# Where weights are asked for, and how side work is slotted, in the backward pass of a gated attention and MLP block

## The chip, the cores and the metric

The kernel runs on one core of one Trainium2 chip. The core has a matrix engine (PE, with weight loads PEld beside it), a vector engine (DVE), a scalar engine (ACT), GpSimd (POOL) and SyncE (SP), which here only issues transfers. Transfers run on 16 DMA engines; SP's transfers show as queue q1, POOL's as q0, ACT's as q10. The metric is the device time of one execution in microseconds, the median of several runs.

## The reference

The forward pass mixes an attention block and an MLP with a scalar gate, for one token of width D = 640:

```python
x = A_x
g = _sigmoid((x * gate_w).sum(-1, keepdims=True))
a = _A_ref(x, A_k_cache, A_v_cache, A_wq, A_wo)
b = _B_ref(x, B_w1, B_b1, B_w2)
return g * a + (1 - g) * b
```

`_A_ref` is attention of one query per head over a cache: 32 heads, 4096 keys, head width 128, bf16. `_B_ref` is `x @ w1 + b1`, then `h * tanh(softplus(h))`, then `@ w2`, with a hidden width of 1728. The kernel must return the output and, for an incoming gradient `grad_out`, the gradients of x, the K cache, the V cache, wq, wo, w1, b1, w2 and gate_w. The K and V caches are 32 MB each and are read once; their gradients are as large and are written once. The gradient of K is an outer product per head (a column ds over the keys, times q), that of V likewise (the column p, times the gradient of the head's output).

## The kernel before

Heads are taken two at a time: a pair n is one tile `Kn` and one tile `Vn` of 128 partitions by 64 by 128, 2 MB each. There are 16 pairs, and the main loop runs `period(n, mid)` for each. Four heads form a group g (two pairs), which has its rows of wo (`wo_g`, 640 KB); eight heads share a slice of wq (`wq_g`, 1280 KB).

A period does this for its pair. PE transposes V in eight chunks (`V(c)`: `transposes`, L606, evicted by ACT to `tT`, L608) and multiplies each with the head's output gradient (`dP(c)`, L615). In the meantime DVE takes the maximum of the scores (L695, the first DVE instruction of a period), ACT makes the exponentials, PE sums them (L710), and PE forms the output O (L732). DVE then makes `part`, `dd` and `dm` (L741, L750, L752), and ACT spreads dm to `ds` (L761). PE multiplies K with dm (L768). The K of the next pair is transposed (`K(c)`) and its scores are formed (`SC(c)`) in the second half of the period. The large DVE work is `outer` (L638): the gradient of V is written over the tile Vn in four quarters (`dv_part`), that of K over Kn in the next period (`dk_part`). After the last quarter POOL issues the store, and SP the load that takes the freed buffer: `load_k(n + 4)` (four buffers) and `load_v(n + 3)` (three buffers). So on SP each K or V load waits until the store of the pair that had the buffer has landed, and what is behind it on SP waits too. Pairs 3 and 9 store V in six pieces (`spread`).

All other work is in a list of named steps with dependencies (`add(name, kind, fn, deps, head)`): kind P for PE, D for DVE, T for anything that is not counted. `slot(h, p, d)` stands at six places of a period, and takes from the list, in its order, up to p steps of kind P and d of kind D whose dependencies were done in an earlier slot; the default is two and one. Step groups:

- `prep_steps(g)` (added by `mid(n)` of the period before the group's first): DVE's products of wo_g with the output gradient (`do_part`, L290), PE's q from wq_g (`qbc`, L301), and the small steps that make the group's vectors.
- `finish_steps(g)` after a group's second pair: the output's product with wo_g (L377), the gradient of wo written over wo_g (`dwo`, L385) and stored by POOL (L386), the query gradient's part of dx from wq_g (`dx`, L396).
- `mlp_steps()`: h and its activation; then, in pieces `CH` of w2's row blocks, the forward product (`b_part`, L496), `dh_part` (L507), the gradient of w2 written over the piece (`dw2_part`, L516, L519); then `dh_cast` and `dh_bc_part` (L540, an ACT copy of dh's rows to all partitions), `dx_part` (L550) and `dw1_part` (L557).

Weights: SP asks for the first two wq_g, the first three wo_g, w1 and the first two pieces of w2 in the beginning. The later two wq_g and five wo_g are asked for on ACT: wq_g by a step after the last `dx` that reads the old one, wo_g by `mid(n)` of odd periods. A wo_g load waits until the store of the gradient that was in its buffer has landed (three buffers). The rows `dh_bc` share their tag, and so their two buffers, with the pieces of w2.

An instruction that waits holds up all that is behind it on its engine, and the order on each engine is that of the program text, slots included.

Of the kernel before, what the change touches and what calls it, by code (L numbers as in the profile page):

```python
# [11 lines left out]
BF16 = mybir.dt.bfloat16  # L12
# [4 lines left out]
def kernel(  # L17
# [39 lines left out]
    FB = FM * P  # L57
    FR = F - FB
    FCN = FM + 1
    CH = [(0, 4), (4, 7), (7, 10), (10, FCN)]  # L60
    NCH = len(CH)
    NT = J // 8
    scale = float(Dh) ** -0.5
# [62 lines left out]
            vts[n] = kv_in.tile([P, J, Dh], BF16, name="Vn", tag="Vn", bufs=VB)  # L126
            nc.sync.dma_start(vts[n][:], Vv[n])

    def load_wq(w, q=nc.sync):
        if w < H // WG:  # L130
            wqs[w] = wts.tile([P, RC, WG * Dh], BF16, name="wq_g", tag="wq_g")
            q.dma_start(wqs[w][:], wq_v[:, :, w * WG * Dh:(w + 1) * WG * Dh])

    def load_wo(g, q=nc.sync):
        if g < NG:
            wos[g] = wts.tile([P, G, D], BF16, name="wo_g", tag="wo_g", bufs=3)
            q.dma_start(wos[g][:], wo_v[g])

    w2cs = {}

    def load_w2(c):
        a, b = CH[c][0], min(CH[c][1], FM)
        w2cs[c] = mlp.tile([P, 4, D], BF16, name="w2c", tag="w2c", bufs=2)
        nc.sync.dma_start(w2cs[c][:, 0:b - a, :], w2_v[:, a:b, :])

    load_wq(0)
# [114 lines left out]
    def add(name, kind, fn, deps=(), head=0):  # L261
        steps.append((name, kind, fn, tuple(deps), head))
# [89 lines left out]
    def finish_steps(g):  # L352
        fs = {}

        def om():
            fs["om"] = small.tile([P, G, G], BF16, name="om", tag="om")
            nc.vector.tensor_tensor(fs["om"][:], o_all[:, g * G:(g + 1) * G].unsqueeze(2).to_broadcast([P, G, G]),
                                    mask4[:].to_broadcast([P, G, G]), ALU.mult)

        def o4():  # L360
            fs["ps"] = gr_ps.tile([P, G], F32, name="o4_ps", tag="gr")
            R = P // G
            for hh in range(G):
                nc.tensor.matmul(fs["ps"][hh * R:(hh + 1) * R, :], lhsT=red4[:], rhs=fs["om"][:, hh, :],
                                 start=True, stop=True)

        def o4c():
            fs["o4"] = small.tile([P, G], F32, name="o4", tag="o4")
            nc.vector.tensor_copy(fs["o4"][:], fs["ps"][:])
            fs["o4b"] = small.tile([P, G], BF16, name="o4b", tag="o4b")  # L370
            nc.vector.tensor_copy(fs["o4b"][:], fs["o4"][:])

        def amm():
            fs["ap"] = gr_ps.tile([P, RC], F32, name="ap_ps", tag="gr")
            for c in range(RC):
                for i in range(G):
                    nc.tensor.matmul(fs["ap"][:, c:c + 1], lhsT=wos[g][:, i, c * P:(c + 1) * P],  # L377
                                     rhs=fs["o4b"][:, i:i + 1], start=(i == 0), stop=(i == G - 1))

        def aadd():  # L380
            nc.vector.tensor_tensor(a_acc[:], a_acc[:], fs["ap"][:], ALU.add)

        def dwo():
            for i in range(G):
                nc.vector.tensor_scalar(wos[g][:, i, :], da_bc[:], fs["o4"][:, i:i + 1], None, ALU.mult)  # L385
            (nc.sync if g == NG - 1 else nc.gpsimd).dma_start(dwo_v[g], wos[g][:])  # L386

        def dqb():
            b_ps = gr_ps.tile([P, G, P], BF16, name="b_ps", tag="gr")
            bcast_rows(b_ps, dq_all[:, g * G:(g + 1) * G], G)  # L390
            nc.scalar.copy(f32v(dq_bc[:, g * GD:(g + 1) * GD]), f32v(b_ps[:].rearrange("p a b -> p (a b)")))

        def dx(rc, c0, c1, slot_i):
            def f():
                w = g // 2
                nc.vector.scalar_tensor_tensor(junk[:, c0:c1], in0=wqs[w][:, rc, c0:c1], scalar=1.0,  # L396
                                               in1=dq_bc[:, w * WG * Dh + c0:w * WG * Dh + c1],
                                               op0=ALU.mult, op1=ALU.mult, accum_out=dxp[:, rc, slot_i:slot_i + 1])
            return f

        n = lambda x: f"{x}{g}"
        add(n("om"), "T", om)
        add(n("dqb"), "P", dqb)
        add(n("o4"), "P", o4, (n("om"),))
        add(n("o4c"), "T", o4c, (n("o4"),))
        add(n("amm"), "P", amm, (n("o4c"),))
        add(n("aadd"), "T", aadd, (n("amm"),))
        add(n("dwo"), "D", dwo, (n("aadd"),))
        for rc in range(RC):
            if g >= NG - 2:  # L410
                add(n(f"dx{rc}_"), "D", dx(rc, (g % 2) * GD, (g % 2 + 1) * GD, g - NG + 2 + NW - 1), (n("dqb"),))
            elif g % 2 == 1:
                add(n(f"dx{rc}_"), "D", dx(rc, 0, WG * Dh, g // 2), (n("dqb"),))
        if g % 2 == 1 and g < NG - 2:
            add(n("wql"), "T", lambda: load_wq(g // 2 + 2, nc.scalar), (n(f"dx{RC - 1}_"),))


    def mlp_steps():
# [107 lines left out]
        def dh_cast():  # L526
            m["dh_bf"] = T("dh_bf", BF16)
            nc.vector.tensor_copy(m["dh_bf"][:], m["dh"][:])
            m["dh_bc"] = mlp.tile([P, F], BF16, name="dh_bc", tag="w2c", bufs=2)

        def dh_bc_part(k):
            def f():
# [33 lines left out]
        for c in range(NCH):  # L566
            add(f"b{c}", "P", b_part(c), ("act2", f"w2_{c}") + ((f"badd{c - 1}",) if c else ()), H0)
            add(f"badd{c}", "T", b_add, (f"b{c}",), H0)
            a, b = CH[c]
            for fc in range(a, b):  # L570
                add(f"dh_{fc}", "D", dh_part(fc), ("act2", f"w2_{c}"), H0)
            add(f"dw2a_{c}", "D", dw2_part(c, a, a + 2), (f"badd{c}",) + tuple(f"dh_{fc}" for fc in range(a, b)), H0)
            add(f"dw2_{c}", "D", dw2_part(c, a + 2, b), (f"dw2a_{c}",), H0)
            if c < 2:
                done[f"w2_{c}"] = -1
            else:
                for k in range(4):
                    add(f"w2w{k}_{c}", "T", lambda: None, (f"w2w{k - 1}_{c}" if k else f"dw2_{c - 2}",), H0)
                add(f"w2l_{c}", "T", lambda c=c: load_w2(c), (f"w2w3_{c}",), H0)
                for k in range(8):  # L580
                    last = k == 7
                    add(f"w2_{c}" if last else f"w2x{k}_{c}", "T", lambda: None,
                        (f"w2x{k - 1}_{c}" if k else f"w2l_{c}",), H0)
        add("dhc", "T", dh_cast, (f"dh_{FCN - 1}", f"dw2_{NCH - 2}"), H0)
        add("dhb0", "P", dh_bc_part(0), ("dhc",), H0)
        add("dhb1", "P", dh_bc_part(1), ("dhc",), H0)
        for rc in range(RC):
# [89 lines left out]
    def period(n, mid):  # L677
# [29 lines left out]
            nc.scalar.activation(pairs(e[hp, :, k]), own(S, k, hp), ACT.Exp, bias=negM[hp], scale=1.0)  # L707
        V(3)
        dP(1)
        nc.tensor.matmul(Z, lhsT=ones_bf[:], rhs=e[:].rearrange("p j k -> p (j k)"), start=True, stop=True)  # L710
        zs = small.tile([P, 2], F32, name="zs", tag="zs")
        nc.vector.reduce_sum(zs[:], Z.rearrange("p (j k) -> p k j", k=2), axis=AX.X)
        rz = st["rz"] = small.tile([P, 2], F32, name="rz", tag="rz")
        nc.vector.reciprocal(rz[:], zs[:])
        dk_part(n - 1, 2)
        V(4)
        dP(2)
        slot(2 * n)
        p_bf = st["p"] = small.tile([P, J, 2], BF16, name="p_bf", tag="p_bf", bufs=2)
        for k, hp in HS:  # L720
            nc.scalar.activation(p_bf[hp], e[hp, :, k].unsqueeze(2).to_broadcast([HP, J, 2]), ACT.Copy,
# [3 lines left out]
        dk_part(n - 1, 3)  # L725
        V(6)
        dP(4)
        slot(2 * n)
        V(7)
        dP(5)  # L730
        for j in range(J):
# [2 lines left out]
            if j == J // 2 - 1:  # L734
                dP(6)
        dP(7)
        slot(2 * n, 2, 2)
        part = small.tile([P, 1], F32, name="part", tag="part")
        pj = f32v(junk[:])[:, 0:J]
        for k, hp in HS:  # L740
# [10 lines left out]
        for k, hp in HS:  # L751
            nc.vector.scalar_tensor_tensor(pairs(dm[hp, :, k]), in0=own(DP, k, hp), scalar=dd[hp],  # L752
                                           in1=pairs(p_bf[hp, :, 0]), op0=ALU.subtract, op1=ALU.mult)
        dv_part(n, 1)
        mid(n)
        nc.vector.tensor_tensor(o_all[:, 2 * n:2 * n + 2], O[:, 0:2], rz[:], ALU.mult)
        ds = st["ds"] = small.tile([P, J, 2], BF16, name="ds_bf", tag="ds_bf", bufs=2)
        SC(0)
        K(2)
        for k, hp in HS:  # L760
            nc.scalar.copy(ds[hp], dm[hp, :, k].unsqueeze(2).to_broadcast([HP, J, 2]))  # L761
        dv_part(n, 2)
        slot(2 * n + 1)
        SC(1)
        K(3)
        dv_part(n, 3)
        for j in range(J):
            nc.tensor.matmul(DQ, lhsT=kts[n][:, j, :], rhs=dm[:, j, :].unsqueeze(1).to_broadcast([P, W // 2, 2]),  # L768
                             start=(j == 0), stop=(j == J - 1))
            if j == J // 2 - 1:  # L770
                SC(2)
                K(4)
                slot(2 * n + 1)
                SC(3)
                K(5)
        SC(4)
# [34 lines left out]
    def mid(n):  # L811
        g = n // 2
        if n % 2 == 0 and g + 1 < NG:
# [1 line left out]
            steps.clear()  # L815
            prep_steps(g + 1, 2 * n + 1)
            steps.extend(rest)
        if n % 2 == 1:
            assert g == 0 or f"dwo{g - 1}" in done
            if g:  # L820
                load_wo(g + 2, nc.scalar)
        if n == NP - 2:
            for rc in range(RC):
                add(f"dwq{rc}", "D", dwq_make(rc), (f"dqb{NG - 2}",), 2 * n + 1 + (rc + 1) // 2)
                add(f"dwqs{rc}", "T", lambda rc=rc: dwq_store(rc), (f"dwq{rc}",), 2 * n + 1)

    for n in range(NP):
        period(n, mid)
        if n % 2 == 1:
            mlp_left = steps[:]  # L830
            steps.clear()
            finish_steps(n // 2)
            steps.extend(mlp_left)
# [78 lines left out]
```

## Time and profile before

| | us |
|---|---|
| median of 8 runs | 416.01 (414.9 to 417.65) |
| the profiled execution | 415.71 |
| its span, first to last instruction | 413.9 |

| engine | busy us (share of the span) |
|---|---|
| PE | 295.0 (71%) |
| PEld | 262.8 (63%) |
| DVE | 309.3 (75%) |
| ACT | 201.4 (49%) |
| POOL | 32.6 (8%) |

The granted clock of the matrix engine was 0.895 in the mean. The transfers by queue, with packets, bytes and the time of their packets as a share of 16 engines' span:

```profile
q1 hardware_dynamic: 10208, 87.51, 52.0%
q0 software_dynamic: 7040, 70.64, 41.5%
q10 hardware_dynamic: 2092, 5.91, 4.0%
```

The costliest groups of DVE, which carries the outer products and most of the side work (line, engine, operation, written tile from read tiles with their shapes, count, then busy us and mean ns of one, then the idle time just before them and what ended most of it):

```profile
L638 DVE TENSOR_TENSOR Vn<-p_bf,qd 128x2048 bf16<-128x2048 bf16 x64 | 78.0, 1220 | 1.0
L638 DVE TENSOR_TENSOR Kn<-ds_bf,qd 128x2048 bf16<-128x2048 bf16 x64 | 77.5, 1218 | 0.9
L290 DVE SCALAR_TENSOR_TENSOR junk<-wo_g,da_bc 128x640 bf16<-128x640 bf16 x32 | 26.3, 821 | 15.5 <-DMA wo_g<-in_A_wo_dram 13.8
```

In the page's slice rows one digit or number stands for a fortieth of the span (10.3 us). In the list of waits a line says which instruction waited for what, then the us in total, the number of times, and the longest.

### The profile page before, as it was taken

The page shows a single profiled execution, that of the slowest core. Times are in us where ns is not written, and L with a number is a line of the kernel's source. Part 1 is how long each engine was busy: PE and PEld are TensorE (multiplying, and loading weights), DVE is VectorE, ACT ScalarE, POOL GpSimd, SP SyncE. Part 2 cuts the span into 40 slices and gives each one's busy share as a digit, 9 for nine tenths or more (in the row PEclk, how much of TensorE's full clock was granted, in tenths as well). Part 3 has the DMA queues.
Part 4 walks back from the last instruction along what each step waited for, and adds up shares of the span by engine and source line. Part 5 has one row for each costly group of instructions (what it writes and reads, how often), then busy time and mean ns, then how long its engine had stood idle before and what let it go on. Part 6 is the DMA issues. An engine that isn't in the chain of part 4 may idle for free.

```text
span 413.9 us, 13164 instructions
## 1 busy us (share of the span) xinstructions
PE 295.0 (71%) x5665; PEld 262.8 (63%) x5672; DVE 309.3 (75%) x736; ACT 201.4 (49%) x451; POOL 32.6 (8%) x72
## 2 busy tenths in 40 slices
PE   1799788686788868537977788836887778978410
PEld 0578788586676758427866677725776667868300
DVE  3318766885499995807769969992799999989983
ACT  1475646372464735404755365705747455737100
POOL 1000100011200000101000102211000010001000
PEclk9899999999698977858999889986999989999755
DMA  8999999999999999998999999999999999998997
GB/s 304 423 415 398 421 412 429 426 429 426 420 415 382 392 415 426 426 401 311 388 355 432 422 420 316 409 356 425 423 380 393 422 414 415 421 405 360 403 420 286
DMA packets 19398, 164.90 MB, mean 398 GB/s; under 512 B 2300, under 2 KB 3004, under 8 KB 11404
## 3 DMA queue, kind: packets, MB, share of 16 engines
q1 hardware_dynamic: 10208, 87.51, 52.0%
q0 software_dynamic: 7040, 70.64, 41.5%
q10 hardware_dynamic: 2092, 5.91, 4.0%
q8 instruction: 44, 0.72, 0.7%
q14 instruction: 14, 0.11, 0.1%
HBM read 82.03 MB, written 82.03 MB: 396 GB/s over the span
## 4 chain that ended last, share of the span: by engine, by line
issue 36%; DMA 25%; DVE 22%; PE 9%; ACT 3%; POOL 2%; SPq 1%; POOLq 0%; ACTq 0%; DVEq 0%
DMA Kn<-in_A_k_cache_dram 9%; DMA Vn<-in_A_v_cache_dram 7%; DVE Vn L638 5%; DVE Kn L638 5%; DMA out_dram<-w2c 5%; PE tr L606 3%; DMA out_dram<-Kn 3%; DVE junk L396 2%; ACT tT L608 2%; DVE junk L550 2%; DMA wq_g<-in_A_wq_dram 2%; PE sB L768 1%; PE sA L615 1%; DVE junk L290 1%; DVE dwq_t L793 1%
## 5 line engine op out<-in xcount | busy, mean ns | idle before, releaser
L608 ACT COPY tT<-tr 128x512 f32<-128x512 f32 x256 | 144.9, 588 | 121.3 <-PE tr L606 106.2
L615 PEld LDWEIGHTS <-tT 128*128 128x128 bf16 x2048 | 81.1, 99 | 40.9 <-ACT tT L608 34.2
L606 PE MATMUL tr<-ident_f,Kn 128*128 128x128 f32 x512 | 88.3, 300 | 3.8 <-DMA Kn<-in_A_k_cache_dram 1.9
L606 PE MATMUL tr<-ident_f,Vn 128*128 128x128 f32 x512 | 78.8, 284 | 0.0
L638 DVE TENSOR_TENSOR Vn<-p_bf,qd 128x2048 bf16<-128x2048 bf16 x64 | 78.0, 1220 | 1.0
L638 DVE TENSOR_TENSOR Kn<-ds_bf,qd 128x2048 bf16<-128x2048 bf16 x64 | 77.5, 1218 | 0.9
L615 PE MATMUL sA<-qd,tT 128*128 128x48 bf16 x1024 | 49.1, 188 | 23.7 <-ACT tT L608 22.7
L606 PEld LDWEIGHTS tr<-ident_f,Vn 128*128 128x128 f32 x512 | 57.0, 145 | 9.4 <-PE sB L615 7.9
L606 PEld LDWEIGHTS tr<-ident_f,Kn 128*128 128x128 f32 x512 | 60.1, 152 | 4.3 <-issue 2.2
L615 PE MATMUL sB<-qd,tT 128*128 128x48 bf16 x1024 | 47.0, 184 | 2.4 <-issue 1.1
L290 DVE SCALAR_TENSOR_TENSOR junk<-wo_g,da_bc 128x640 bf16<-128x640 bf16 x32 | 26.3, 821 | 15.5 <-DMA wo_g<-in_A_wo_dram 13.8
L768 PEld LDWEIGHTS <-Kn 128*128 128x128 bf16 x1024 | 33.4, 100 | 6.7 <-issue 6.1
L768 PE MATMUL sB<-dm,Kn 128*128 128x48 bf16 x1024 | 33.8, 189 | 4.9 <-DVE dm L752 3.1
L732 PE MATMUL sA<-em,Vn 128*128 128x48 bf16 x1024 | 30.9, 183 | 0.7 <-issue 0.7
L695 DVE TENSOR_REDUCE m<-sA 64x1 f32<-64x64 f32 x32 | 7.1, 221 | 30.1 <-PE sA L615 29.8
L732 PEld LDWEIGHTS <-Vn 128*128 128x128 bf16 x1024 | 28.0, 96 | 0.8 <-issue 0.8
L396 DVE SCALAR_TENSOR_TENSOR junk<-wq_g,dq_bc 128x1024 bf16<-128x1024 bf16 (+1 forms) x25 | 25.1, 1006 | 0.2
L301 PE MATMUL q_ps<-wq_g,cols_bf 128*128 128x512 bf16 x33 | 12.1, 489 | 11.5 <-DMA wq_g<-in_A_wq_dram 10.6
L662 POOL DMA_DIRECT2D out_dram<-Vn x13 | 7.1, 545 | 166.4 <-DVE Vn L638 87.1
L741 DVE SCALAR_TENSOR_TENSOR junk<-sB,em 64x64 f32<-64x64 f32 x32 | 7.1, 222 | 17.4 <-PE sB L615 8.4
L650 POOL DMA_DIRECT2D out_dram<-Kn x15 | 8.4, 560 | 134.9 <-DVE m L325 43.8
L745 PE MATMUL sB<-ident_f,part 128*128 128x128 f32 x16 | 5.0, 310 | 14.8 <-DVE junk L741 14.6
(150 smaller groups left out, 265.5 us busy)
## 6 DMA issues: line engine op xcount, KB each, us to landing
Kn<-in_A_k_cache_dram SPq DMA_DIRECT2D x16, 2048.0 KB, 13.7
Vn<-in_A_v_cache_dram SPq DMA_DIRECT2D x16, 2048.0 KB, 16.9
out_dram<-Kn POOLq DMA_DIRECT2D x15, 2048.0 KB, 15.5
out_dram<-Vn POOLq DMA_DIRECT2D x13, 2048.0 KB, 15.3
out_dram<-wo_g POOLq DMA_DIRECT2D x7, 640.0 KB, 15.3
out_dram<-dwq_t SPq DMA_DIRECT2D x4, 896.0 KB, 10.8
wo_g<-in_A_wo_dram ACTq DMA_DIRECT2D x5, 640.0 KB, 14.0
wq_g<-in_A_wq_dram SPq DMA_DIRECT2D x2, 1280.0 KB, 6.3
```

The costliest lines, as they stand in the source:

```text
L290: nc.vector.scalar_tensor_tensor(junk[:, 0:D], in0=wos[g][:, i, :], scalar=1.0, in1=da_bc[:], op0=ALU.mult, op1=ALU.mult, accum_out=gp["do ...
L301: nc.tensor.matmul(q_ps[:], lhsT=x_bf[:, rc:rc + 1].to_broadcast([P, P]), rhs=wq[:, rc, off:off + GD], start=(rc == 0), stop=(rc == RC - 1))
L396: nc.vector.scalar_tensor_tensor(junk[:, c0:c1], in0=wqs[w][:, rc, c0:c1], scalar=1.0, in1=dq_bc[:, w * WG * Dh + c0:w * WG * Dh + c1], op ...
L550: nc.vector.scalar_tensor_tensor(junk[:, 0:F // 2], in0=w1_sb[:, rc, a:b], scalar=1.0, in1=m["dh_bc"][:, a:b], op0=ALU.mult, op1=ALU.mult, ...
L606: nc.tensor.transpose(tp[:, t, :], flat[:, k * P:(k + 1) * P], ident_f[:])
L608: nc.scalar.copy(sb[:].rearrange("p a b -> p (a b)"), tp[:].rearrange("p a b -> p (a b)"))
L615: nc.tensor.matmul(out[:, 4 * k:4 * k + W], lhsT=tb[:, t, par, :], rhs=vec[:, par].rearrange("p k r -> p (k r)").unsqueeze(1).to_broadcast ...
L638: nc.vector.tensor_tensor(dst[:, a:b, :].rearrange("p j (a b) -> p j a b", b=2), col[:, a:b, :].unsqueeze(2).to_broadcast([P, n, Dh // 2, 2]),
L650: ring(n).dma_start(dKv[n], kts[n][:])
L662: ring(n).dma_start(dVv[n], vts[n][:])
L732: nc.tensor.matmul(O, lhsT=vts[n][:, j, :], rhs=e[:, j, :].unsqueeze(1).to_broadcast([P, W // 2, 2]), start=(j == 0), stop=(j == J - 1))
L768: nc.tensor.matmul(DQ, lhsT=kts[n][:, j, :], rhs=dm[:, j, :].unsqueeze(1).to_broadcast([P, W // 2, 2]), start=(j == 0), stop=(j == J - 1))
```

## The change

- The pieces of w2 are three row blocks each (five pieces) instead of four, three, three and four (four pieces), and their buffers are smaller.
- `load_wq` and `load_wo` always issue on SP. The wo_g load of an odd period stands ahead of the period, hence ahead of that period's K load on SP, instead of in `mid(n)`.
- `dh_bc` has a tag and a buffer of its own, and `dh_cast` depends only on the last dh, not on the gradient of the last but one piece of w2.
- Four slots take two steps of DVE instead of one, so that all six take two. The third slot of a period moves from ahead of `part` to behind `dm`, and `mid(n)` stands right behind it, ahead of the second quarter of dV.
- `V(4)` goes ahead of the sum of exponentials, and `K(2)` ahead of `SC(0)`.

```diff
-    CH = [(0, 4), (4, 7), (7, 10), (10, FCN)]
+    CH = [(0, 3), (3, 6), (6, 9), (9, 12), (12, FCN)]
...
-    def load_wq(w, q=nc.sync):
+    def load_wq(w):
...
-            q.dma_start(wqs[w][:], wq_v[:, :, w * WG * Dh:(w + 1) * WG * Dh])
+            nc.sync.dma_start(wqs[w][:], wq_v[:, :, w * WG * Dh:(w + 1) * WG * Dh])
-    def load_wo(g, q=nc.sync):
+    def load_wo(g):
...
-            q.dma_start(wos[g][:], wo_v[g])
+            nc.sync.dma_start(wos[g][:], wo_v[g])
...
-        w2cs[c] = mlp.tile([P, 4, D], BF16, name="w2c", tag="w2c", bufs=2)
+        w2cs[c] = mlp.tile([P, 3, D], BF16, name="w2c", tag="w2c", bufs=2)
...
-            add(n("wql"), "T", lambda: load_wq(g // 2 + 2, nc.scalar), (n(f"dx{RC - 1}_"),))
+            add(n("wql"), "T", lambda: load_wq(g // 2 + 2), (n(f"dx{RC - 1}_"),))
...
-            m["dh_bc"] = mlp.tile([P, F], BF16, name="dh_bc", tag="w2c", bufs=2)
+            m["dh_bc"] = mlp.tile([P, F], BF16, name="dh_bc", tag="dh_bc")
...
-            add(f"dw2a_{c}", "D", dw2_part(c, a, a + 2), (f"badd{c}",) + tuple(f"dh_{fc}" for fc in range(a, b)), H0)
-            add(f"dw2_{c}", "D", dw2_part(c, a + 2, b), (f"dw2a_{c}",), H0)
+            add(f"dw2a_{c}", "D", dw2_part(c, a, a + 1), (f"badd{c}",) + tuple(f"dh_{fc}" for fc in range(a, b)), H0)
+            add(f"dw2_{c}", "D", dw2_part(c, a + 1, b), (f"dw2a_{c}",), H0)
...
-        add("dhc", "T", dh_cast, (f"dh_{FCN - 1}", f"dw2_{NCH - 2}"), H0)
+        add("dhc", "T", dh_cast, (f"dh_{FCN - 1}",), H0)
...
         dP(1)
+        V(4)
         nc.tensor.matmul(Z, lhsT=ones_bf[:], rhs=e[:].rearrange("p j k -> p (j k)"), start=True, stop=True)
...
         dk_part(n - 1, 2)
-        V(4)
         dP(2)
-        slot(2 * n)
+        slot(2 * n, 2, 2)
...
         dP(4)
-        slot(2 * n)
+        slot(2 * n, 2, 2)
...
         dP(7)
-        slot(2 * n, 2, 2)
         part = small.tile([P, 1], F32, name="part", tag="part")
...
+        slot(2 * n, 2, 2)
+        mid(n)
         dv_part(n, 1)
-        mid(n)
...
+        K(2)
         SC(0)
-        K(2)
...
         dv_part(n, 2)
-        slot(2 * n + 1)
+        slot(2 * n + 1, 2, 2)
...
                 K(4)
-                slot(2 * n + 1)
+                slot(2 * n + 1, 2, 2)
...
-        if n % 2 == 1:
-            assert g == 0 or f"dwo{g - 1}" in done
-            if g:
-                load_wo(g + 2, nc.scalar)
...
     for n in range(NP):
+        g = n // 2
+        if n % 2 == 1:
+            assert g == 0 or f"dwo{g - 1}" in done
+            if g:
+                load_wo(g + 2)
         period(n, mid)
```

## The prediction

> **What bounds the kernel now.** I read the page first: busy shares, then the forty slices. No engine is full (DVE, the busiest, 75%), while the DMA row stands at 8 or 9 in every slice.
>
> ```profile
> DMA  8999999999999999998999999999999999998997
> GB/s 304 423 415 398 421 412 429 426 429 426 420 415 382 392 415 426 426 401 311 388 355 432 422 420 316 409 356 425 423 380 393 422 414 415 421 405 360 403 420 286
> DMA packets 19398, 164.90 MB, mean 398 GB/s; under 512 B 2300, under 2 KB 3004, under 8 KB 11404
> ```
>
> So the transfers bound it: 164.90 MB at the rate of a good slice would need 390 us (164.90 / 0.423), and the rest of the span is the start, the end and the slices that dip. Next I cut the span at the dips. Columns: stretch and length, busy us of PE, PEld, DVE, ACT, POOL, granted clock, DMA share, GB/s.
>
> ```profile
> 130.00:140.00 10.00, 9.04 (x197) 8.32 (x197) 9.79 (x25) 5.95 (x15) 1.09 (x2) 1.00 1.00 357
> 140.00:185.00 45.00, 28.88 (x513) 25.42 (x514) 29.73 (x69) 18.15 (x41) 2.67 (x5) 0.76 1.01 423
> 185.00:195.00 10.00, 7.92 (x151) 7.38 (x149) 5.92 (x16) 3.92 (x11) 0.53 (x1) 0.84 0.79 288
> ...
> 205.00:220.00 15.00, 11.91 (x238) 10.99 (x237) 10.67 (x22) 9.25 (x21) 0.53 (x1) 1.00 1.00 369
> ...
> 245.00:255.00 10.00, 7.70 (x167) 6.95 (x167) 9.40 (x24) 6.05 (x13) 0.53 (x1) 1.00 0.89 303
> ...
> 265.00:280.00 15.00, 7.25 (x159) 6.54 (x157) 13.35 (x34) 3.56 (x8) 1.66 (x3) 0.86 1.01 364
> ...
> 300.00:320.00 20.00, 15.78 (x322) 13.92 (x319) 19.40 (x41) 11.40 (x26) 1.06 (x2) 1.00 0.98 385
> ...
> 370.00:380.00 10.00, 7.29 (x135) 6.87 (x135) 9.45 (x20) 5.25 (x12) 1.95 (x3) 1.00 0.85 347
> ```
>
> Against 423 GB/s a stretch loses its length times (1 - rate/423): 1.6, 3.2, 1.9, 2.8, 2.1, 1.8 and 1.8 us in the order shown (the second row is the reference), and 0.4 more in 195 to 205 (405 GB/s). Together 15.6 us: all that a change of order can win, since it moves as many bytes. Why do they dip? I asked for the waits inside two windows (170 to 192, 268 to 290).
>
> ```profile
> DVE junk L290 <- DMA wo_g<-in_A_wo_dram: 13.8, 1, 13.8
> PE q_ps L301 <- DMA wq_g<-in_A_wq_dram: 10.6, 1, 10.6
> ```
>
> ```profile
> ACT dh_bc L540 <- DMA out_dram<-w2c: 11.9, 1, 11.9
> PEld L615 <- ACT tT L608: 11.2, 1, 11.2
> ```
>
> In both the computing engines stand still; no dK or dV store is asked for, hence no load into the buffer that it would free, and some us later the DMA runs dry. A third kind: ACT blocks on an issue of its own, and its copies behind it wait.
>
> ```profile
> 104.79 0.37 ACTq L137 DMA_DIRECT2D wo_g<-in_A_wo_dram  x1
> 105.25 0.58 ACT L608 COPY tT<-tr 128x512 f32<-128x512 f32 x1 [5.15 <-DMA out_dram<-wo_g]
> ```
>
> Why did the wq_g load, issued on ACT at 143.2, land only at 182? The DMA view of 144 to 182 says it (queue: packets, MB, share):
>
> ```profile
> q0 software_dynamic: 731, 7.73, 48.2%
> q1 hardware_dynamic: 453, 6.64, 41.0%
> q10 hardware_dynamic: 726, 1.66, 11.1%
> ```
>
> q10, ACT's queue, got as many packets as q0 and a fifth of the bytes. I lastly timed the periods by the reduce of L695: they start at 24.8, 42.9, 63.1, 87.1, 113.3, 137.0, 161.1, 194.8, 214.5, 242.0, 261.8, 293.1, 313.7, 337.0, 356.0 and 376.3. The long ones, period 6 (33.7 us) and 10 (31.3), hold the two stalls; an undisturbed one is 18 to 24 us.
>
> **What the Trainium skill says.** "DMA: Bandwidth & Descriptors", Queues, rings and completion order: each DMA engine goes round robin over the queues that have work, one packet each. The counts above agree (731 against 726). Same page, Anatomy of one DMA: DMA engines don't wait on semaphores, the wait sits on the issuing sequencer before dispatch. The 5.15 us above agree. Same page, Issuing engines are not separate DMA queues: a second issuer brings no bandwidth; the total here stays near 423 with three queues at work.
>
> **The change part by part.**
>
> Weights to SyncE. Two wq_g and five wo_g loads leave ACT for SP's queue q1. ACT's 9.9 us of blocking (three waits in the list of waits) go. On q1 a load follows the K and V loads in line. wq_g of groups 4 and 5 is asked for behind V of pair 7, at about 149 (V of pair 7 was issued at 149.2). It needs V's time to land (16.9 us, median) and some 3 us of its own (1.31 MB at 423), so about 168; the first use was tried at 171.6 and will come a few us sooner without ACT's stalls. I take the 10.6 and 13.8 us waits as gone but for a rest of 1 or 2 us; from the trace it could be 0 or the full 10. SP is in order, so each added issue can hold what is behind it. A wo_g load waits for the wo_g store two groups back (136.2 for the load in period 5); that store follows the dV store (133.1) on POOL's queue, whose end SP has already waited for with V. The K load behind waits for the dK store of 144.6, which is later. So nothing behind is held beyond 1 to 2 us; the issue itself takes 0.33 to 0.43. wq_g's own release, five DVE reads, is long past. The w2c loads wait for w2c stores one to two periods old: nothing.
>
> dh rows in their own buffer. The 11.9 us wait on the w2c store goes, and with it ACT's 11.2 us for PE. The rows also come out behind the ds copies on ACT. What is late next: DVE, which idles only 8.3 us there.
>
> DVE work two to a slot, and the third slot behind dm. By instruction count the total is the same to 3 rows; only the place changes. Prices from rows of the before, with the accumulator read: L396 1.30, L507 0.96, L290 0.90, L550 1.13, L385 and L516 0.38, L557 0.66. In the built order period 4 gets 2 L507, 1 L396 and 1 L516 more (3.6 us), period 8 1 L507, 1 L396 and 3 L516 (3.4), period 12 1 L396 and 1 L550 (2.4); periods 9 and 13 lose 6 to 7 us each, and fall under what PE and ACT need anyway (18 to 20 us, as periods 0, 7 and 13 show), so that isn't all given back. In period 4 some 3.5 us of it stand ahead of the dV store. Cover: period 4 was filled by DVE (23.0 of 23.7 us), so there is none on DVE; the cover is the queued transfers. I charge 0.4 us each, 1.2 in all; 0 if the queues stay full, 3.5 each if they are dry. The slot behind dm brings dm, ds and PE's dQ forward by two L396 at most; worth nothing where the DMA is the bound.
>
> V(4) ahead of the Z matmul: PE waits there 9.4 us in all for ACT's exp, 0.6 a period; hidden by the DMA as well. w2 by threes: one piece more, same bytes. On POOL's queue two w2c stores now stand ahead of a dK and a dV store, 0.49 MB each, 1.2 us later for those; inside the cover of the queued transfers, so nothing; without it 2.4.
>
> **Sum.** Of each dip I take what its cause carries. 185 to 205: 3.2 of 3.6 (the weights stall). 205 to 220: 1.6 of 1.9 (period 7's stores came late from it). 245 to 255: 1.2 of 2.8 (two stores lay far apart, 234.3 and 249.8, in a period of 27.4 us that period 8's added work doesn't shorten). 265 to 280: 1.0 of 2.1 (it begins ahead of the dh wait). 300 to 320: 1.4 of 1.8 (follows from that wait). 370 to 380: 0.6 of 1.8 (loads are over, period 13 is lighter). 130 to 140: nothing (period 4 grows). Sum 9.0, less 1.2, so 7.8. The profiled span 413.9 becomes 406.1; its execution took 415.71, 1.8 beyond the span, so 407.9; the median shown is 416.01, 0.3 more: 408. A measurement of this kernel tells about 0.3% (1.2 us) from no change.
>
> **Rivals.**
> Full recovery, chance 0.22. Without their stalls (5, 4, 13, 4 and 10 us in periods 3, 5, 6, 8 and 10) the periods add up to 336 of 372 us, well under what the DMA needs; then compute waits for loads and the queues never empty: 416.0 - 15.6 = 400.4. Against it: K loads let PE wait only 1.9 us so far, and bunched work dries queues locally.
> The gaps move, chance 0.10. Stores now come in bunches after periods 4, 8 and 12 and the DMA dries there instead: 9.0 won, three times 3 lost, 416.
> Slower, chance 0.18: wq_g is the head of q1 while POOL's stores fill q0. Its 2 KB packets, 40 on each engine, each let one q0 packet by. From the rows above a q10 packet took 0.09 us and a q0 packet 0.40 (share x 38 us x 16 / packets), so 40 pairs take 20 us, not 3, and K and V loads stand behind it for 17 us, twice. It also lands too late again, so of the gains only the dh parts (2.4) stay. If a quarter of 34 us reaches the end: 416.0 - 2.4 + 1.2 + 8.5 = 423. It decides once wq_g lands more than 22 us after its issue (149 to 171). For it: the 39 us on q10. Against it, the window 58 to 68, where wq_g ran on q1 beside stores:
>
> ```profile
> q1 hardware_dynamic: 720, 2.50, 63.1%
> q0 software_dynamic: 118, 1.67, 39.3%
> ```
>
> There q1 took six packets to one of q0, so its small packets did not have to wait in turn.
>
> **How the numbers follow.** Forecast 0.50 (own range 403 to 413, from 13 us of recovery to 3, bursts taken off), full recovery 0.22, gaps move 0.10, slower 0.18. Faster: 0.50 + 0.22 + 0.02 of the third. Same: 0.06 of the third. Slower: 0.18 + 0.02. The range 400 to 419 leaves out most of the slower case and the edge of the full recovery.
>
> **What would show it.** Right: no q10 load in mid run; ACT never waits on out_dram<-wo_g or w2c; q_ps waits under 2 us for wq_g; periods 6 and 10 near 20 to 24 us, period 4 near 27; 185 to 220 above 400 GB/s; a new dip, if any, behind periods 4, 8 or 12. Wrong: wq_g takes over 22 us to land, PE waits for Kn or Vn by several us, or SP's waits on wo_g stores put K loads back; then the place of the weights was the mistake.

## The result and the profile after

| | before | after |
|---|---|---|
| median, us | 415.99 (32 runs, 412.94 to 420.06) | 420.26 (11 runs, 418.34 to 423.22) |
| ratio | | 1.0111 (95% interval 1.0081 to 1.0140) |
| the profiled execution, us | 415.71 | 422.25 |
| its span, us | 413.9 | 420.4 |

The ratios here and below are of runs in the fast state; of the experiments one run of four in e1 and five of twelve in e10, over 1.5% above the fastest of their kernel, count as slow and are left out of the ratio, not of the median.

The changed kernel is 1.1% slower. DVE does the same work (308.8 us busy, 309.3 before) and the same bytes move. The difference of the spans, 6.5 us, is time in which the transfers run below their rate. The page's slice row and packet line of the changed kernel:

```profile
GB/s 303 433 409 399 424 406 425 424 429 426 418 424 352 416 430 421 428 423 426 423 428 405 315 419 357 371 424 369 365 289 323 376 422 313 424 414 300 427 403 306
DMA packets 19525, 164.89 MB, mean 392 GB/s; under 512 B 2332, under 2 KB 3164, under 8 KB 11532
```

The dips that the kernel before had between 186 and 217 us (311, 388 and 355) are gone, and new ones stand in the second half. The windows of the changed kernel (columns as before):

```profile
185.00:195.00 10.00, 9.13 (x190) 8.04 (x189) 6.14 (x11) 7.74 (x19) 0.53 (x1) 1.00 1.00 418
205.00:220.00 15.00, 11.14 (x189) 10.50 (x189) 11.03 (x24) 6.81 (x14) 1.61 (x3) 0.77 1.02 430
...
255.00:270.00 15.00, 4.81 (x75) 4.50 (x75) 5.63 (x9) 5.45 (x12) 0.57 (x1) 0.82 1.02 349
...
290.00:320.00 30.00, 21.62 (x434) 19.39 (x434) 28.79 (x63) 16.27 (x38) 3.97 (x7) 0.99 0.84 309
```

Against the 423 GB/s of the prediction the last row loses 8.1 us (30 times 1 - 309/423). The kernel before ran at 394 GB/s there and lost 2.1. So a loss of 6.0 us, near the whole 6.5, lies in this stretch, behind period 10. The rest is a balance: 185 to 220 us wins 5.8, while 230 to 240 (297 GB/s, 431 before) and 350 to 360 (307, 419 before) together lose as much. Timed by L695 as in the prediction, period 10 now takes 40.6 us instead of 31.3, while periods 3 and 5 fell from 26.2 to 19.2 and from 24.1 to 18.3. What period 10 waits for is in the list of waits of the changed kernel, 140 to 300 us:

```profile
PE bp L496 <- DMA w2c<-in_B_w_dram: 18.3, 2, 15.4
DVE junk L507 <- DMA w2c<-in_B_w_dram: 16.6, 2, 14.5
...
PE q_ps L301 <- DMA wq_g<-in_A_wq_dram: 13.0, 1, 13.0
...
DVE junk L290 <- DMA wo_g<-in_A_wo_dram: 10.5, 1, 10.5
```

ACT no longer waits for a store, but the two waits for weights in period 6 are there again (13.0 and 10.5; before 10.6 and 13.8), and the longest wait for a piece of w2 has grown from 2.9 to 15.4 us. The chain of waits of the changed kernel, 240 to 320 us, shows where it starts:

```profile
244.72 0.33 SPq L127
245.09 1.38 SPq L132
246.58 29.05 DMA w2c<-in_B_w_dram
275.68 1.23 PE bp L496 x10
```

SP issues V, right behind it wq_g (L132), right behind that the fifth piece of w2: 160 KB that take 29 us to land. PE and DVE stand still, no gradient is stored, no buffer comes free; 15 us after the stall's end the rate begins to fall, and between 310 and 320 it is some 205 GB/s. Why a load takes so long is in the DMA view of the other wq_g load (issued at 147.58; its packets run over 17.7 us, from 158.3, nearly all from about 160), 162 to 172 us:

```profile
q0 software_dynamic: 253, 3.66, 86.0%
q1 hardware_dynamic: 272, 0.56, 14.3%
```

Turn for turn: 272 packets of SP's queue beside 253 of POOL's, but 0.56 MB beside 3.66. A q0 packet took 0.54 us (86.0% of 10 us times 16 engines, over 253), a q1 packet 0.08. The loads issued behind wq_g wait through this. In the answer for 160 to 176 us two K loads are asked for. The one whose landing is known, asked for at 175.64 as wq_g's last packets went, found the loads put off by it still ahead of it and landed after 29.1 us (15.3 is the median over the whole run):

```profile
Kn<-in_A_k_cache_dram SPq DMA_DIRECT2D x2, 2048.0 KB, 29.1
```

### The profile page after: what moved, and what is told of

Read it like the earlier page. It is cut to its first block, busy times and chain, and to the rows that moved or that the text cites. A ratio compares the mean times of both kernels' runs of the same rounds, so it can differ in the third digit from the quotient of the medians.

```text
span 420.4 us, 13173 instructions
## 1 busy us (share of the span) xinstructions
PE 297.8 (71%) x5665; PEld 266.3 (63%) x5672; DVE 308.8 (73%) x737; ACT 198.9 (47%) x451; POOL 32.6 (8%) x73
## 2 busy tenths in 40 slices
DMA packets 19525, 164.89 MB, mean 392 GB/s; under 512 B 2332, under 2 KB 3164, under 8 KB 11532
## 4 chain that ended last, share of the span: by engine, by line
DVE 25%; issue 22%; DMA 22%; PE 21%; ACT 6%; POOL 2%; SPq 1%; ACTq 0%; POOLq 0%; DVEq 0%
DMA w2c<-in_B_w_dram 14%; PE tr L606 8%; DVE Kn L638 6%; DVE Vn L638 5%; ACT tT L608 4%; DMA out_dram<-Kn 4%; PE sA L732 3%; DMA out_dram<-Vn 3%; DVE junk L290 2%; PE sA L615 2%; DVE junk L550 2%; PE sB L768 2%; DVE junk L396 2%; PE sB L615 1%; DMA vec_rows<-in_gate_w_dram 1%
## 5 line engine op out<-in xcount | busy, mean ns | idle before, releaser
L608 ACT COPY tT<-tr 128x512 f32<-128x512 f32 x256 | 143.1, 588 | 139.3 <-PE tr L606 129.6
L606 PE MATMUL tr<-ident_f,Kn 128*128 128x128 f32 x512 | 84.4, 294 | 0.5 <-DMA Kn<-in_A_k_cache_dram 0.5
L606 PE MATMUL tr<-ident_f,Vn 128*128 128x128 f32 x512 | 84.2, 297 | 0.5 <-issue 0.5
L606 PEld LDWEIGHTS tr<-ident_f,Vn 128*128 128x128 f32 x512 | 60.9, 152 | 0.9 <-issue 0.8
L606 PEld LDWEIGHTS tr<-ident_f,Kn 128*128 128x128 f32 x512 | 58.7, 149 | 1.0 <-PE sB L615 0.6
L615 PE MATMUL sA<-qd,tT 128*128 128x48 bf16 x1024 | 47.2, 186 | 8.0 <-ACT tT L608 4.8
L290 DVE SCALAR_TENSOR_TENSOR junk<-wo_g,da_bc 128x640 bf16<-128x640 bf16 x32 | 26.3, 821 | 12.3 <-DMA wo_g<-in_A_wo_dram 10.5
L732 PE MATMUL sA<-em,Vn 128*128 128x48 bf16 x1024 | 31.9, 185 | 0.0
L732 PEld LDWEIGHTS <-Vn 128*128 128x128 bf16 x1024 | 29.0, 97 | 0.1
L695 DVE TENSOR_REDUCE m<-sA 64x1 f32<-64x64 f32 x32 | 7.1, 221 | 24.3 <-PE sA L615 24.1
L301 PE MATMUL q_ps<-wq_g,cols_bf 128*128 128x512 bf16 x33 | 12.7, 502 | 16.2 <-DMA wq_g<-in_A_wq_dram 13.0
L507 DVE SCALAR_TENSOR_TENSOR junk<-w2c,dm,db_bc 128x640 bf16<-128x640 bf16 x13 | 11.4, 881 | 16.7 <-DMA w2c<-in_B_w_dram 16.6
L301 PEld LDWEIGHTS <-cols_bf 128*128 128x128 bf16 x40 | 4.3, 116 | 20.4 <-issue 18.9
## 6 DMA issues: line engine op xcount, KB each, us to landing
Kn<-in_A_k_cache_dram SPq DMA_DIRECT2D x16, 2048.0 KB, 15.3
Vn<-in_A_v_cache_dram SPq DMA_DIRECT2D x16, 2048.0 KB, 16.3
out_dram<-Vn POOLq DMA_DIRECT2D x13, 2048.0 KB, 13.3
wq_g<-in_A_wq_dram SPq DMA_DIRECT2D x4, 1280.0 KB, 26.6
```

The lines of the kernel that those rows point to most:

```text
L290: nc.vector.scalar_tensor_tensor(junk[:, 0:D], in0=wos[g][:, i, :], scalar=1.0, in1=da_bc[:], op0=ALU.mult, op1=ALU.mult, accum_out=gp["do ...
L301: nc.tensor.matmul(q_ps[:], lhsT=x_bf[:, rc:rc + 1].to_broadcast([P, P]), rhs=wq[:, rc, off:off + GD], start=(rc == 0), stop=(rc == RC - 1))
L507: nc.vector.scalar_tensor_tensor(junk[0:r, 0:D], in0=w2p(fc), scalar=m["dm"][0:r, fc:fc + 1], in1=db_bc[0:r, :], op0=ALU.mult, op1=ALU.mul ...
L606: nc.tensor.transpose(tp[:, t, :], flat[:, k * P:(k + 1) * P], ident_f[:])
L608: nc.scalar.copy(sb[:].rearrange("p a b -> p (a b)"), tp[:].rearrange("p a b -> p (a b)"))
L615: nc.tensor.matmul(out[:, 4 * k:4 * k + W], lhsT=tb[:, t, par, :], rhs=vec[:, par].rearrange("p k r -> p (k r)").unsqueeze(1).to_broadcast ...
```

## The experiments

The first theory was the place of the weights: wq_g at the head of SP's queue, with 2 KB packets that go one for one with the stores, so that it and all behind it come late. Its rivals: the denser slots bunch DVE's work or bring the uses of w2 ahead of their loads; the w2 part costs; or the gaps only moved. Each experiment ran beside the kernel before, whose medians then were 415.71 to 416.64 us. Differences in us below are taken from 415.99 and 420.26, and carry that spread. "Queue" below is the DMA queue.

| run | what it is | us | ratio (95% interval) |
|---|---|---|---|
| e1 | before + both weights on SP | 424.53 | 1.0144 (1.0032 to 1.0256) |
| e2 | changed, both weights back on ACT | 416.19 | 1.0001 (0.9967 to 1.0035) |
| e3 | changed, wq in long rows | 411.41 | 0.9887 (0.9804 to 0.9970) |
| e4 | changed, wq_g asked ahead of V | 416.05 | 1.0006 (0.9980 to 1.0031) |
| e5 | before + slots and order | 408.26 | 0.9804 (0.9728 to 0.9880) |
| e6 | before + dh buffer and w2 by threes | 410.83 | 0.9868 (0.9811 to 0.9924) |
| e7 | before + wo_g on SP | 409.90 | 0.9842 (0.9785 to 0.9898) |
| e8 | changed, wq_g back on ACT | 411.33 | 0.9882 (0.9824 to 0.9940) |
| e9 | e8, w2 asked earlier | 403.89 | 0.9707 (0.9669 to 0.9746) |
| e10 | before + wq_g on SP | 418.22 | 1.0017 (0.9991 to 1.0044) |
| e11 | e5 + wo_g on SP | 405.71 | 0.9739 (0.9707 to 0.9770) |
| e12 | e6 + wo_g on SP | 406.04 | 0.9751 (0.9717 to 0.9785) |
| e13 | changed, w2 asked earlier | 410.14 | 0.9863 (0.9803 to 0.9922) |
| e14 | changed, wo_g back on ACT | 424.07 | 1.0200 (1.0123 to 1.0276) |

**e1 and e2: the weights alone, and all but the weights.**

```diff
# e1, against before (load_wo in mid goes)
-            add(n("wql"), "T", lambda: load_wq(g // 2 + 2, nc.scalar), ...
+            add(n("wql"), "T", lambda: load_wq(g // 2 + 2), ...
+                load_wo(g + 2)          # ahead of period(n, mid)
# e2, against the changed kernel: the same three edits backwards
```

> The kernel before with one part of the change: all weights asked for on SP. Theory T (the 2 KB packets of wq_g at the head of SP's queue go one for one with the 16 KB packets of POOL's stores, so a wq_g load takes 25 us and more whichever queue it is on, and what stands behind it is late): wq_g still lands 25 us or more after its issue, the 10 us wait of q_ps stays within 4 us, ACT's waits on wo_g stores (9.9 us) are gone, and the time is 413 to 419. Rival R (the place of the weights is harmless, DVE work bunched in periods 4, 8 and 12 makes the change slow): wq_g lands in under 20 us and the time falls to 411 or less.

> The changed kernel with the weights back on ACT, at the places of the kernel before. T: the 14.5 us wait for the fifth piece of w2, which stood behind wq_g on SP, is gone, the 11.9 us wait for dh is gone, the wait for wq_g of about 10 us stays: 408 to 416. R: the bunched DVE work stays, so it is as slow as the changed kernel, 419 or more.

The weights' new place alone costs 1.4%, and without it the rest of the change is worth nothing. In e1 wq_g was issued at 162.2, behind a K load on SP (at 137.0 on ACT in e7, which is e1 but for this), and PE waited 28.1 us for it; periods 6 and 10 took 47.9 and 36.6 us, and the periods behind them ran at 272 and 341 GB/s. So the place of the weights is bad, but it isn't all: the other parts should have brought something in e2, and DVE waits there 8.4 us in all for w2, ACT 15.6 for wo_g's stores.

**e3: the same bytes of wq in rows of 10 KB.**

```diff
+    wq_l = A_wq.rearrange("(w r) c -> w (r c)", w=H // WG).rearrange("w (p x) -> w p x", p=P)
-            nc.sync.dma_start(wqs[w][:], wq_v[:, :, w * WG * Dh:(w + 1) * WG * Dh])
+            nc.sync.dma_start(wqs[w][:].rearrange("p a b -> p (a b)"), wq_l[w])
```

> The changed kernel with each wq_g load of the same 1280 KB read as 10 KB runs in place of 2 KB ones, so in a fifth of the packets; wq's elements are then taken in another arrangement, so q and what follows from it are others. Nothing else moves. T: wq_g lands in 20 us or less, the waits for wq_g (13.0 us) and for the fifth piece of w2 (14.5 us) fall under 3 us each, and the time is 410 or less. R: wq_g's packets don't matter for the time, 417 or more.

The test of the mechanism: place, order and bytes stay, only the number of packets changes (17477 instead of 19525). The kernel leaves out the right arrangement of wq's elements, so its q is another; only its time is read here. 8.9 us of the changed kernel's time go (420.26 to 411.41); the forecast of at most 410 was just missed. From first packet to last the two wq_g loads take 8.6 and 5.7 us instead of 17.7 and 13.3, and PE no longer waits for them at all. The DMA view of e3, its lines on landing (the view has it for one of the four wq_g loads, the last; 26.6 in the changed kernel):

```profile
wq_g<-in_A_wq_dram SPq DMA_DIRECT2D x4, 1280.0 KB, 17.3
w2c<-in_B_w_dram SPq DMA_DIRECT2D x4, 480.0 KB, 26.2
```

The second line is the next problem: pieces of w2, whose packets are 3840 bytes (1280 for the fifth piece). It is the median of two landings, one from the start of the kernel (22.3 us) and one in mid run (30.2), and PE still waits 14.4 us for them.

**e4: wq_g ahead of V on SP.**

```diff
# in dx, behind its last instruction; the wql step goes
+                if rc == RC - 1 and g % 2 == 1 and g < NG - 2:
+                    load_wq(g // 2 + 2)
```

> The changed kernel with the wq_g load issued right behind the last read of the old one, so that it stands ahead of the V load on SP, about 12 us earlier. T: it still takes about 25 us, but the wait for it falls under 4 us; the wait for the fifth piece of w2 gets shorter by some 10 us; 407 to 414. R: 417 or more.

Missed: 416.05, only 4.2 us won, above the forecast. Issued at 135.0, 12.6 us sooner, wq_g of group 4 landed after 37.5 us. Its packets ran over 25.1 us instead of 17.7, so it was ready only some 4 us sooner; PE still waited 7.9 us, and V now stood behind it.

**e5, e6 and e7: the other parts alone.** e5 is the kernel before with the changed `period`; e6 has `CH`, the tiles of three rows, the tag and the dependency of `dh_cast`; e7 moves `load_wo` alone.

```diff
# e6, besides the w2 and dh lines of the change: w2 asked for after 1 slot, used after 6
-                for k in range(4):
+                for k in range(1):
-                for k in range(8):
+                for k in range(6):
# e7
-                load_wo(g + 2, nc.scalar)
+                load_wo(g + 2)          # ahead of period(n, mid)
```

> The kernel before with the slots part alone (two DVE steps to every slot, the third slot behind dm, V(4) and K(2) moved). Theory T2 (the change has two costs, wq_g at the head of SP's queue and DVE work bunched in periods 4 and 8, and the bunching eats what the earlier work gives): 413 to 418, wq_g asked for some 10 us earlier and its wait gone, but dips under 330 GB/s behind periods 4, 8 or 12. Rival S (the slots are a gain by themselves, and only the weights cost): 411 or less.

> The kernel before with dh rows in their own buffer and w2 by threes; the waits counted in slots ahead of and behind a w2 load are 1 and 6 in place of 4 and 8, since the fifth piece would not be done in time with one DVE step to a slot. If the 11.9 us wait of ACT for a w2c store was on the path: 409 to 413. If the transfers go on during that wait and it only stands where another would (rival H): 414 to 417.

> The kernel before with the five wo_g loads alone on SP ahead of the K load; wq_g stays on ACT. T2: wo_g's 5 KB packets don't hold up SP's queue much, ACT's 9.9 us of waits go, wq_g is asked for as before and q_ps waits about 10 us: 411 to 415. Rival (any weight on SP's queue costs): 418 or more.

Each is a gain: 2.0, 1.3 and 1.6%. The rival in which denser slots cost falls: they are the best single part. In e5 wq_g, still on ACT, is asked for at 132.4 instead of 143.2, because `dx` is done sooner, and PE doesn't wait for it. e7 holds a lesson on reading waits. Its list of waits has a longer one than the kernel before (10.6):

```profile
PE q_ps L301 <- DMA wq_g<-in_A_wq_dram: 19.4, 1, 19.4
```

Its window of that period, 40 us long:

```profile
150.60:190.60 40.00, 19.51 (x360) 16.81 (x360) 19.32 (x48) 12.10 (x26) 2.14 (x4) 0.74 1.01 424
```

PE was busy for half of it, and the queues still moved 424 GB/s; the period behind it lost little (398). A stall of the engines costs only what it leaves undone by the time the queues have emptied. Here the engines had run ahead in periods 3 to 5 (ACT's stalls are gone), so that enough was queued; this is a reading, not a test. e12 shows the same: PE waits 21.7 us, period 6 takes 42.8 us at 426 GB/s, and the kernel is 2.5% faster. A period 6 that is as long but starts 8.5 us later (e10, below) or starts as early but is 47.9 us long (e1) leaves 289 and 272 GB/s behind it; both have wq_g on SP, so the lead by itself isn't isolated.

**e8 and e9: wq_g alone back on ACT, and then w2 sooner.**

```diff
# e8, against the changed kernel
-            add(n("wql"), "T", lambda: load_wq(g // 2 + 2), ...
+            add(n("wql"), "T", lambda: load_wq(g // 2 + 2, nc.scalar), ...
# e9, besides e8: w2 asked for after 1 slot, used after 11 more
-                for k in range(4):
+                for k in range(1):
-                for k in range(8):
+                for k in range(11):
```

> The changed kernel with wq_g alone back on ACT; wo_g stays on SP. T2: wq_g is asked for at about 133 and lands before its use, nothing stands behind it on SP, waits for w2 pieces of 5 to 8 us stay: 409 to 414, under the changed kernel by 6 or more. Rival (wo_g on SP or the slots make the cost): 417 or more.

> The changed kernel with wq_g back on ACT, and each later w2 piece asked for three slots earlier, its use left where it was (waits counted in slots 1 and 11 in place of 4 and 8). T2: the waits for w2 pieces (10.4, 6.6 and 4 to 5 us with wq_g back on ACT alone) fall under 3 us each, and the time is 403 to 409. Rival (those waits are covered by queued transfers): 410 to 412, as with wq_g back on ACT alone.

e8 wins 8.9 us of the changed kernel's time, as much as the long rows of e3. The load is no faster on ACT's queue (40.6 us for the first), but it is asked for at 128.7, 18.8 us sooner than in the changed kernel, where it comes behind V on SP, and nothing else stands behind it. It isn't quite in time: PE waits 7.0 us for it. e9 wins 7.4 more and is faster than both kernels. Three slots are worth more than they seem, since on SP a piece of w2 comes out right behind a K or V load that waits for a store. The fifth piece on SP, in e8 and then in e9, where it stands ahead of that V load and comes out 24 us sooner:

```profile
249.94 0.33 SPq L127 DMA_DIRECT2D Vn<-in_A_v_cache_dram  x1
250.38 1.02 SPq L144 DMA_DIRECT2D w2c<-in_B_w_dram  x1
...
225.99 0.33 SPq L122 DMA_DIRECT2D Kn<-in_A_k_cache_dram  x1
226.42 0.37 SPq L144 DMA_DIRECT2D w2c<-in_B_w_dram  x1
```

The page of e9:

```profile
GB/s 295 430 406 403 422 414 416 426 430 423 429 418 394 360 418 437 419 427 425 425 426 429 421 426 414 418 394 413 421 421 413 407 426 419 410 389 375 421 418 297
DMA packets 19526, 164.90 MB, mean 409 GB/s; under 512 B 2332, under 2 KB 3164, under 8 KB 11532
```

Between the start and the end only one slice stands below 375. Its waits, 140 to 300 us:

```profile
PE q_ps L301 <- DMA wq_g<-in_A_wq_dram: 6.6, 2, 4.6
...
PE bp L496 <- DMA w2c<-in_B_w_dram: 2.9, 1, 2.9
```

**e10, e11 and e12: wq_g on SP by itself, and pairs of the good parts.** The edits are those above: e10 is the first line of e1, e11 is e5 and e7, e12 is e6 and e7.

> The kernel before with the two later wq_g loads alone on SP; wo_g stays on ACT. T2: wq_g lands 25 us or more after its issue, q_ps waits 20 us or more, loads stand behind it on SP, and the time is 419 to 428. Rival (it costs only together with wo_g behind it on the same queue): 414 to 418.

> The kernel before with the slots part and with wo_g on SP; wq_g on ACT, w2 in its four pieces and dh rows in their shared buffer. If the parts add up where DMA still has dips to fill: 401 to 406. If each removes the same dips: 406 to 410.

> The kernel before with dh rows in their own buffer, w2 by threes (waits of 1 and 6 slots) and wo_g on SP; wq_g on ACT, slots as before. If the parts add up: 402 to 406. If each removes the same dips: 407 to 411.

e10 missed: 418.22 in the median of 12 runs, 0.5% above the kernel before beside it, and wide (414.32 to 425.07); its ratio in the table tells no change. Its trace shows the same pattern as e1 (PE waits 19.6 us for wq_g, period 6 takes 40.3 us, the period behind runs at 289 GB/s), but what it costs isn't the same each time. e1 differs from e7 by the same edit: 0.9842 against 1.0144. e11 and e12 join the gain of wo_g to that of the slots or the w2 part (0.9739 and 0.9751); both win less than the sum of their parts, though the intervals just leave room for it.

**e13 and e14: what stands behind wq_g.** Open by then was what passes wq_g's slowness on: the w2 piece, the wo_g load, or K and V.

```diff
# e13, against the changed kernel: the two edits of e9, wq_g stays on SP
# e14, against the changed kernel: wo_g back on ACT, in mid
-                load_wo(g + 2)
+                load_wo(g + 2, nc.scalar)
```

> The changed kernel with wq_g still on SP, and only the later w2 pieces asked for three slots earlier, so that their waits of 18.5 and 16.6 us go and the fifth piece stands ahead of wq_g of group 5 instead of behind it. If what is lost stands in the queue behind wq_g whatever it is (K and V loads, wo_g) and the w2 waits are a second cost that adds up: 410 to 416 (420.3 less about the 7.4 us that the same edit brought with wq_g on ACT). If wq_g on SP costs only by holding up the w2 piece behind it: 403 to 408, as with wq_g on ACT. If the w2 waits are cover for stalls that come anyway: 418 to 422.

> The changed kernel with wq_g on SP and only wo_g back on ACT. If wq_g costs by holding up K, V and w2 loads: 416 to 423, and PE still waits over 8 us for wq_g. If wq_g costs mainly by holding up the wo_g load behind it (DVE's wait of 10.5 us): 409 to 413, and the wo_g wait is gone. ACT waits again on wo_g stores, some 10 us in all.

In e13 the fifth w2 piece is issued at 232.7, ahead of wq_g, and every wait for w2 is gone. The list of waits of e13:

```profile
PE q_ps L301 <- DMA wq_g<-in_A_wq_dram: 16.4, 2, 8.7
DVE junk L290 <- DMA wo_g<-in_A_wo_dram: 16.3, 2, 10.1
```

Weights are waited for twice, longer in all than in the changed kernel, and still 10.1 us are won (410.14). But the edit moves all three later pieces of w2, and with wq_g on ACT it won 7.4 (e8 to e9), so most of the gain doesn't come from freeing a piece that stood behind wq_g. 410 to 416 was the forecast for two costs that add up, 403 to 408 that for a wq_g that costs only by the w2 piece behind it: the first came. Nor do the traces show a wait for K or V: between 140 and 300 us no instruction of PE or DVE waits for either, in the changed kernel or in e13.

e14 shows that wo_g behind wq_g isn't the main cost: its wait is gone, yet the time doesn't fall (424.07, a little above the forecast), and PE waits 12.7 us for wq_g and 9.8 for w2. ACT waits for wo_g's stores again, 7.8 us in all. If that costs the whole 6.1 us that e7 won, freeing wo_g is worth 2.3 at most (an estimate).

## Why the prediction was wrong

It said 408 with a range of 400 to 419; the time is 420.26. One path through the runs adds the parts one by one: slots 0.9804 (e5), wo_g on SP 0.9739 (e11), dh and w2 by threes 0.9882 (e8), wq_g on SP 1.0111 (the changed kernel). The first two win 2.6%; the last two lose 1.4 and 2.3% of the kernel before.

**wq_g on q1: the step that failed.** "It needs V's time to land ... and some 3 us of its own ... so about 168." V did pass by about 160, but wq_g then went by turns until the stores ran out at about 173 (172 to 174: 249 packets of q1, 22 of q0), and was there at about 176. In place of 3 us stand 17.7, and "10.6 and 13.8 us waits as gone" became 13.0 and 10.5. e3 shows the cause: larger rows, same place, no wait.

The slower rival had this mechanism, with the right threshold (over 22 us; 26.6 and about 29 measured) and nearly the time (423). That time is luck in part: its sum charged the slots 1.2 us, which won 7.7 (e5), left out what w2 costs, and let K and V pay, for which no engine waits. It got 0.18 because of the window 58 to 68, which was misread. The share of packets was taken over 10 us, but wq_g's went for the most part between 60 and 64 (535 of 640), just while q0 was dry. Cut to 60 to 62 us, the DMA view of the kernel before says:

```profile
q1 hardware_dynamic: 345, 0.71, 92.6%
q0 software_dynamic: 11, 0.05, 6.0%
```

Eleven packets of q0 were there to take turns with; the next store was issued at 60.04 and its packets came at 64. The window 144 to 182 on q10, which was in hand, was the fair sample: stores queued, and one for one. The Trainium skill's sentence that the prediction had cited ("DMA: Bandwidth & Descriptors", Queues, rings and completion order) holds in both windows; what the trace has to supply is whether the other queue has work.

**What stands behind it.** "So nothing behind is held beyond 1 to 2 us" looked at SP's waits, not at the ring that SP feeds. In the changed kernel the fifth w2 piece behind wq_g took 29 us, and the dip of 290 to 320 us follows the wait for it (309 GB/s; 409 in e13, without that wait). In the rival it was K and V that paid; no engine waits for them. Over the whole run wq_g on SP and the late w2 are two costs that nearly add up: asking for w2 earlier wins 10.1 us (e13), taking wq_g off SP wins 8.9 (e8), both 16.4 (e9). The 2.7 us by which both fall short of the sum are less than the intervals of the four runs leave open (some 4 us, an estimate from them). So with w2 asked early wq_g on SP still costs 6.2 us (e13 to e9). In the traces that stands beside longer waits for wq_g itself (16.4 us in e13, 6.6 in e9) and for the wo_g behind it (16.3 and 6.8); how the cost divides between them isn't settled.

**w2.** "The w2c loads wait for w2c stores one to two periods old: nothing" and "by threes ... nothing" were the second failure, in the company of the slots. The program counts the delay between asking for a piece and using it in slots (four and eight). In us it is what SP leaves: in e8 the three later pieces came out 12.6, 17.9 and 9.2 us ahead of their first use, and took 18.2, 22.9 and 14.1 us to be there; in the kernel before, two pieces had 30.4 and 16.6 us. A period has six slots in both kernels, so it isn't the count that shrank. Asked three slots earlier, the pieces had 24.1, 20.0 and 30.3 us (e9). Added to slots and wo_g, the part costs 5.6 us (e11 to e8); asked three slots sooner it costs nothing (e11 to e9: 1.8 us less, inside the intervals). Alone, in the old slots and with delays of its own, it won 5.2 us (e6), twice the 2.4 that the sum gave the dh wait.

**The slots.** They were charged 1.2 us and won 7.7 (e5). The 0.4 us per bunch may be right; period 4 grew to 26.9 us as forecast (near 27). The new dip in period 8 (230 to 235 us, 223 GB/s) looks like the one foreseen for bunched work, but it goes with the late w2: 230 to 240 us runs at 410 GB/s with the slots alone (e5), at 297 in the changed kernel and 279 in e8, and at 418 and 426 once w2 is asked for earlier in these two (e13, e9). What was left out is what sooner steps ask for: wq_g 10.8 us earlier.

**What held.** The transfers bound it: the loss is one of their rate. ACT's blocking ended, periods 3 and 5 shrank, and 185 to 220 us runs at 426 GB/s where above 400 was asked for. The wo_g part wins (e7). That the gain was in reach is shown by e9: 12.1 us below the kernel before, between the forecast and the full recovery.

## What to carry to other kernels

A load of small packets beside busy queues should be timed by turns, not by bytes: its packets per engine times the packet time of the queue that it shares with (here 40 times 0.54, some 22 us, an estimate; 17.7 were measured, since the stores ran out on the way), and all that is queued behind it on its ring waits too. Long rows (e3) and another issuer that could ask sooner (e8) won 8.9 us each; asking sooner on the same queue won 4.2 (e4). Before a rate is read from a window, check that the other queue had work all through it. Where a scheduler counts a load's lead in slots, the lead in us is what the issuer's own waits leave of it, so the delays belong to the change and are to be read from the trace again after it.

## What the runs showed of the hardware

- 1.31 MB of wq_g took 6.3 us from issue to landing at the start, when no store was queued. In mid run, with stores queued, its packets alone ran over 17.7 and 13.3 us on SP's queue, 33.7 and 13.3 on ACT's (the kernel before), and 8.6 and 5.7 us in 10 KB rows.
- The Trainium skill ("DMA: Bandwidth & Descriptors", Issuing engines are not separate DMA queues) has it that a second issuing engine saves only the time of issuing. In bandwidth that agrees with this case: 423 GB/s with loads on two issuers (140 to 185 us of the kernel before), 425 with all on one (the changed kernel). But the choice of the issuer was worth more than the time of issuing: with wq_g alone on another issuer the time fell from 420.26 to 411.33. There the load was asked for 18.8 us sooner, and no other load stood behind it; the two weren't tested apart.
- A full DMA share isn't a full rate. In 255 to 270 us of the changed kernel the engines were busy all the time (1.02) at 349 GB/s, with small packets on both queues (q0 765 for 3.09 MB, q1 786 for 2.13 MB). In 162 to 172 us, with small packets on q1 alone, it was 425. That the packets are the cause wasn't tested by itself.
